# A fused layer norm, linear attention and ReLU block: w1 held in three column parts, w2 and wo loaded inside the last chunk, and two groups of sums moved

## The chip, the cores and the metric

The kernel runs on one core of a Trainium2 chip. The metric is the device time of one execution in microseconds (us). The kernel before took 221.77 us in the median of 3 runs (221.74 to 221.9). One more execution was profiled; every row of a profile below comes from that one.

The engines are named as in the profile: PE is TensorE's matmul, PEld its weight load, DVE is VectorE, ACT is ScalarE, POOL is GpSimd, SP is SyncE, which here only issues DMAs. "SPq" and "ACTq" are the DMA issues of SP and of ACT. Each engine works through its own list of instructions in order; a waiting instruction holds up everything behind it in that list.

## The reference

x has 2048 tokens of D = 640 channels. H = 32 heads of 20 channels, Dff = 1728.

```python
xn = layernorm(x)
q, k, v = split(xn @ wqkv)                # 32 heads of 20 each
phi = lambda t: where(t > 0, t + 1, exp(t)) + 1e-6
kv  = einsum("bhsd,bhse->bhde", phi(k), v)
z   = phi(k).sum(over tokens)
num = einsum("bhqd,bhde->bhqe", phi(q), kv)
den = einsum("bhqd,bhd->bhq", phi(q), z) + 1e-6
s   = (num / den) @ wo
g   = silu(relu(xn @ w1) @ w2)
out = x + s * g
```

## The kernel before, in words

**Tiles and chunks.** The tokens are 16 tiles of 128 (`t`), and four chunks of 512 (`j`). xn is kept with tokens in the partitions (`xn`) and, transposed, with channels in the partitions (`xnT`; chunk 0 has its own copy, `xcT`). From tile 4 on the transposed copy is a DMA transpose that SP issues (L497), right behind the tile's normalisation.

**The main loop (L854).** For each chunk there is a written list of blocks, `plans[j]`: an H block (`H_block`, L579) computes 128 columns of relu(xn @ w1) for the chunk, a Q block (`Q_block`, L558) 128 columns of phi(q). Each is 5 matmuls of 128 x 512. An H block's result goes through ACT (L586); a Q block's through ACT (exponential, L567) and two operations of DVE (L568, L570). At fixed positions `n` of the list other work is hung in:

- `lnat`: the statistics of a token tile (L426, L430 on DVE, then two small POOL operations, L432 and L434, that make 1/sqrt as `rsy`), and one position later its normalisation (L445 on DVE) and its transposed copy. Tiles 8 to 11 are treated in chunk 1, tiles 12 to 15 in chunk 2, at n = 0, 2, 4 and 6.
- `kat`: the key product of a token tile (`K_mm`, L507, 10 matmuls), two ACT operations (L524) and `K_fin` on DVE (L540, L542), which gives phi(k), `pk`. Tile 12's key product stands at n = 6 of chunk 2.
- `zfrom`: from which position on one addition to the running sum z (L518 on POOL, 128 x 640 in f32) is issued per position, for each `pk` that is ready. Before: from 9, 11 and 10 in chunks 0, 1 and 2.
- In chunk 3: the split of z in two bf16 halves (`z_split`, L674 and L676 on POOL), `z_col` (L681 on PE), the 64 columns of w1 left over (`H_half`, L601), and `den` (L694 on PE, then L698 and the reciprocal L703 on DVE, and four DMAs that write the reciprocal, spread over 20 channels per head, to a DRAM scratch `scr`, L709).

**The memory product.** Instead of kv directly, the kernel forms G = xn^T @ pk over all tokens (640 x 640). 128 rows of it are plain matmuls (L1154); the other 512 rows are two products of 2 x 2 blocks with seven block products instead of eight each (`seven`, L798; matmuls in L786). These need sums of the blocks of pk, called T1 to T4 (`g_T1` to `g_T4`), and of the blocks of xn, S1 to S4 for each of the two products (`g_S(0, i)`, `g_S(1, i)`). All of them are DVE operations of one helper line, L732: T of 128 x 2560, S of 128 x 1024. T3 and S3 are written over parts of pk and xn that the plain matmuls L1154 read. L821 is a DVE operation inside each `seven`.

**After it.** G is turned into kv with wv (`kv_group`, L926, evacuated by L936 on DVE), then multiplied with wo (`W_block`, L948), copied by ACT (L952) and put in place by small DMAs (L959, by SP for even blocks, by ACT for odd ones). Between these stand the first products with w2 (`U_sub`, L983). The gate's silu on ACT is L992 and L998. Before the attention output of a token tile (L1098) comes, `divide` (L725 on DVE) multiplies phi(q) by the reciprocals read back from `scr` (`load_recip`, L720, five loads of 512 KB into `Rr[0..4]`). Six more pairs of token tiles then go through `seven` with w2, the attention product, L1086, the sum with x and the store.

**Shared room.** `reg5` holds w1 and later w2. `reg7` holds the tiles of x, later the S sums of the second product, later wo. `regE` holds the work tiles of K and Q, then z's halves and the reciprocal, and later `Rr[0..3]`. Before the change w1 is one array of 5 x 1728 per partition, so that any chunk of w2 overlaps columns of all parts of w1: w2 was loaded after the last H work of the loop (`extra=[lastW1]`).

**Order and waits.** `Sched` records every operation in program order, with the keys it reads and writes; it appends it to its engine's list and derives the waits. `hz(keys)` gives the earlier users of keys whose room is used anew. A DMA waits in the list of the engine that issues it. The SP list after the loop was, before: the four stores of the reciprocal, two large and two small loads of w2, the five loads of the reciprocal, six loads of wo (`extra=[lastG]`, behind the last matmul of the second `seven`), the DMAs L959, the reload of x.

Of the kernel before, what the change touches and what calls it, by code (L numbers as in the profile page):

```python
# [208 lines left out]
def bass_recurrent_scan__linear_attn_block__dense_activation_relu__prompt_kernel(  # L209
# [9 lines left out]
    Bb, S, D = A_x.shape  # L219
# [49 lines left out]
    reg5 = nc.alloc_sbuf_tensor("reg5", [P, R5], bf)  # L269
    w1_sb = reg5[:, 0:C * FF].rearrange("p (c n) -> p c n", c=C)  # L270
    w2_sb = reg5[:, 0:NK * D].rearrange("p (c n) -> p c n", c=NK)
# [81 lines left out]
    TS = 2  # L353
    FC = [0, 4 * P, 7 * P, FF]

    def w1_part(f):
        return 0 if f < 4 else 1 if f < 7 else 2

    def w1_load(i, E):
        w_load(w1_sb[:, :, FC[i]:FC[i + 1]], B_w1[:, FC[i]:FC[i + 1]], ("w1", i), E=E)  # L360

# [217 lines left out]
    def H_block(j, f):  # L579
        b = nextb()  # L580
        src, keys = hsrc(j)
        a = sc.group("PE", [(lambda eng, k=k: eng.matmul(ps[b], lhsT=w1_sb[:, k, P * f:P * (f + 1)],  # L582
                                                         rhs=src[:, k, :],
                                                         start=(k == 0), stop=(k == C - 1))) for k in range(C)],
                     R=[("w1", w1_part(f))] + keys, W=[("ps", b)])
        sc.op("ACT", lambda eng: eng.activation(out=hT[:, f, schunk(j)], in_=ps[b], func=ACTF.Relu),  # L586
              R=[("ps", b)], W=[("hT", j, f)])
        return a

    def H_half(jp):  # L590
# [5 lines left out]
        for k in range(C):  # L596
            for u in range(2):
                src = hsrc(2 * jp + u)[0]
                for q in range(2):
                    r = 64 * u + 32 * q  # L600
                    fns.append(lambda eng, k=k, src=src, q=q, r=r: eng.matmul(  # L601
                        ps[b][r:r + 32, :], lhsT=w1_sb[:, k, NF * P + 32 * q:NF * P + 32 * (q + 1)],
                        rhs=src[:, k, :], start=(k == 0), stop=(k == C - 1), tile_position=(0, r)))
# [85 lines left out]
    def den():  # L689
# [14 lines left out]

        sc.op("DVE", frec, R=[("denS",)], W=[("rden",)])
        for i in range(J):
            src = rden[H * i:H * (i + 1), :].unsqueeze(1).to_broadcast([H, DH, 512])
# [8 lines left out]

    def load_recip():
        ex = hz([("rden",), ("denS",), ("zhi",), ("zlo",)] + ekeys + [("xcT", q, h) for q in range(4) for h in range(2)])
        for m in range(C):
            dma("SP", lambda eng, m=m: eng.dma_start(Rr[m], scr[P * m:P * (m + 1), :]),  # L720
                R=[("scr", i) for i in range(J)], W=[("Rr", m)], extra=ex)
# [37 lines left out]
    def g_Sv(pr, i):  # L759
        if i == 3:  # L760
            return xnh[:, 0:GH, P * (2 * pr + 1):P * (2 * pr + 2)]
        q = {1: 0, 2: 1, 4: 2}[i]
        base = reg6h[:, C * D:] if pr == 0 else reg7h
        return base[:, GH * P * q:GH * P * (q + 1)].rearrange("p (t n) -> p t n", t=GH)

    def g_S(pr, i):
        k0, k1 = slice(P * 2 * pr, P * (2 * pr + 1)), slice(P * (2 * pr + 1), P * (2 * pr + 2))
        xl, xh = [("xn", t) for t in range(GH)], [("xn", t) for t in range(GH, T)]
        A11, A12, A21, A22 = xn[:, 0:GH, k0], xn[:, GH:T, k0], xn[:, 0:GH, k1], xn[:, GH:T, k1]
        ex = hz([("wk", k) for k in range(C)]) if pr == 0 else hz([("xin", q) for q in range(XR)])  # L770
        key = lambda q: ("gS", pr, q)
# [26 lines left out]
    def seven(base, prod, out, mids):  # L798
# [36 lines left out]
        out(21, bd)  # L835

    lastW1 = None
    plans = [
# [6 lines left out]
    for j in range(1, J):  # L845
        ql = list(qs[j])
        for f in range(NF):
            plans[j].append(("h", j, f))
# [3 lines left out]
    lnat = [{}, {0: 8, 3: 9, 6: 10, 9: 11}, {0: 12, 2: 13, 4: 14, 6: 15}, {}]  # L852
    zfrom = [9, 11, 10, 0]
    for j in range(J):  # L854
        for n, item in enumerate(plans[j]):
# [27 lines left out]
            if n >= zfrom[j] and zpend and j < J - 1:  # L883
                z_add()
            if j == 2 and n == 0:
                g_T1()
            if j == 2 and n == 1:
                build_consts()
            if j == J - 1:
# [4 lines left out]
                if 4 <= n < 8:  # L894
                    g_S(0, n - 3)
                if n == 9:
                    z_col()
                    w_load(wv_sb[:, :, :], A_wqkv[:, 2 * D:3 * D], ("wv",), extra=hz([("zacc",)]))
                if n == 11:
                    lastW1 = H_half(0)  # L900
                    lastW1 = H_half(1)
                    den()
                if n == 12:
                    g_T2()
                    g_T4()

    for a in range(2):
        c0, c1 = (0, KH) if a == 0 else (KH, NF)
        dma("SP", lambda eng, c0=c0, c1=c1: eng.dma_start(
            w2_sb[:, c0:c1, :], B_w2[P * c0:P * c1, :].rearrange("(c p) n -> p c n", p=P)),  # L910
            W=[("w2", a)], extra=[lastW1])
    for u in range(2):
        dma("SP", lambda eng, u=u: eng.dma_start(w2_sb[64 * u:64 * (u + 1), NF, :], B_w2[NF * P:FF, :]),
            W=[("w2", 2 + u)], extra=[lastW1])
    load_recip()
    w2keys = [("w2", i) for i in range(4)]

# [234 lines left out]
    for t in range(T):  # L1152
        for a in range(2):
# [106 lines left out]
```

## Time and profile before

| | before |
|---|---|
| median of 3 runs | 221.77 us (221.74 to 221.9) |
| the profiled execution | 221.37 us |
| its span | 220.1 us |
| PE busy | 209.9 us (95%) |
| DVE busy | 146.2 us (66%) |
| ACT busy | 102.8 us (47%) |
| POOL busy | 46.1 us (21%) |
| granted TensorE clock | 1.00 |

The span runs from the first to the last recorded event. A row of the timeline gives start, duration, engine, line, operation, output<-inputs, size and how many instructions are merged in it; in brackets, how long the engine was idle before it and what ended the idle time. The table of waits sums the same brackets. A mean over the span hides where the engines meet: PE is busy 95% of it, and DVE, at 66%, was busy 15.86 of the 16.3 us from 48.7 to 65.0.

### The profile page before, as it was taken

To read this page: it belongs to the slowest core of one execution; us is meant where nothing else is said; L and a number is where in the kernel's file an instruction comes from. 1 tells how busy PE (TensorE), PEld (TensorE's weight loads), DVE (VectorE), ACT (ScalarE), POOL (GpSimd) and SP (SyncE) were. 2 spreads that over 40 slices of the span, in tenths; PEclk is the share of its full clock that TensorE was granted. 3 is DMA by queue.
4 is the path that set the end of the run, shared out by engine and by line. 5 is a ranking of instruction groups with operands and counts; after the bars stand their busy time and mean duration, and the time that the engine had idled before them with its cause. 6 is when DMAs were issued, how large, how long until landed. Compare 5 with 4: busy or idle time off the path is not lost.

```text
span 220.1 us, 3544 instructions
## 1 busy us (share of the span) xinstructions
PE 209.9 (95%) x1402; PEld 129.9 (59%) x1402; DVE 146.2 (66%) x265; ACT 102.8 (47%) x187; POOL 46.1 (21%) x70
## 2 busy tenths in 40 slices
PE   8999999999996899999999996799999999999994
PEld 7755554555542455444457675576777777777773
DVE  3899957789999891386657110995057879575254
ACT  5697575666654466655632333333332323242330
POOL 2278501229759344600000000000000000000001
PEclk9999999999999999999999999999999999999999
DMA  6987593111001120040069999525911111010002
GB/s 216 370 231 162 131 277 66 30 30 30 3 1 30 34 56 3 0 149 3 0 150 222 248 339 388 209 78 171 359 50 61 44 49 58 5 60 31 30 33 89
DMA packets 28438, 24.73 MB, mean 112 GB/s; under 512 B 12037, under 2 KB 27781, under 8 KB 28421
## 3 DMA queue, kind: packets, MB, share of 16 engines
q1 hardware_dynamic: 26335, 21.87, 35.3%
q10 hardware_dynamic: 2086, 2.63, 3.7%
q8 instruction: 11, 0.18, 0.4%
q14 instruction: 6, 0.05, 0.1%
HBM read 15.81 MB, written 5.24 MB: 96 GB/s over the span
## 4 chain that ended last, share of the span: by engine, by line
PE 72%; DVE 15%; DMA 5%; issue 2%; ACT 2%; ACTq 1%; POOL 1%
PE psT L786 23%; PE psT L582 18%; PE psT L1098 9%; PE psT L507 8%; PE psT L560 4%; DMA reg<-in_A_wo_dram 4%; DVE regE L568 3%; DVE pqT L570 3%; PE psT L983 3%; DVE reg L732 2%; PE psT L1154 2%; DVE reg L445 2%; PE psT L396 2%; DVE stats L426 1%; ACT reg L952 1%
## 5 line engine op out<-in xcount | busy, mean ns | idle before, releaser
L582 PE MATMUL psT<-reg 128*128 128x512 bf16 x195 | 46.0, 379 | 0.0
L586 ACT ACTIVATE regH<-psT 128x512 bf16<-128x512 f32 x52 | 30.8, 602 | 17.2 <-PE psT L582 17.2
L786 PE MATMUL psT<-reg 128*128 128x320 f16 (+1 forms) x238 | 34.6, 299 | 0.3 <-DVE psT L821 0.3
L582 PEld LDWEIGHTS psT<-reg 128*128 128x128 bf16 x195 | 18.9, 98 | 21.9 <-issue 0.4
L786 PEld LDWEIGHTS psT<-reg 128*128 128x128 f16 (+1 forms) x238 | 23.2, 98 | 9.6 <-DVE psT L821 0.6
L1091 POOL TENSOR_TENSOR reg<-reg 128x224 bf16<-128x224 bf16 x1 | 0.6, 606 | 124.3 <-DVE reg L1086 124.3
L518 POOL TENSOR_TENSOR wv_sb<-wv_sb,reg 128x640 f32<-128x640 f32 x16 | 23.2, 1450 | 13.4 <-DVE reg L542 12.9
L786 PE MATMUL psT<-reg,regH 128*128 128x320 bf16 (+1 forms) x168 | 24.9, 299 | 0.0
L560 PE MATMUL psT<-reg 128*128 128x512 bf16 x100 | 24.8, 379 | 0.0
L1098 PE MATMUL psT<-reg,pqT 128*128 128x320 bf16 (+2 forms) x165 | 24.2, 295 | 0.0
L998 ACT ACTIVATE wv_sb<-psT 128x320 bf16<-128x320 f32 x20 | 8.7, 437 | 27.9 <-PE psT L786 24.5
L524 ACT ACTIVATE regE<-psT 128x640 bf16<-128x640 f32 x24 | 15.6, 701 | 11.8 <-PE psT L507 11.8
L507 PE MATMUL psT<-reg 128*128 128x320 bf16 x120 | 18.3, 299 | 2.5 <-DMA reg<-reg 2.5
L786 PEld LDWEIGHTS psT<-reg,regH 128*128 128x128 bf16 (+1 forms) x168 | 16.4, 98 | 6.4
L732 DVE TENSOR_TENSOR reg<-reg 128x1024 f16<-128x1024 bf16 (+4 forms) x16 | 16.8, 1066 | 4.2 <-PE psT L1154 4.0
L1098 PEld LDWEIGHTS psT<-reg,pqT 128*128 128x128 bf16 x165 | 16.1, 98 | 5.8
L983 PE MATMUL psT<-reg,regH 128*128 128x320 bf16 x112 | 16.2, 299 | 1.8 <-DMA reg<-in_B_w_dram 1.8
L1086 DVE TENSOR_TENSOR reg<-psT,wv_sb 128x640 bf16<-128x640 f32 (+2 forms) x16 | 11.7, 739 | 9.2 <-PE psT L1098 9.2
L570 DVE SCALAR_TENSOR_TENSOR pqT<-regE 128x512 bf16<-128x512 bf16 x20 | 17.1, 856 | 0.7
L507 PEld LDWEIGHTS psT<-reg 128*128 128x128 bf16 x120 | 11.7, 98 | 9.2 <-DMA reg<-reg 3.0
L568 DVE TENSOR_SCALAR regE<-psT 128x512 bf16<-128x512 f32 x20 | 13.5, 677 | 5.2 <-ACT regE L567 5.1
L560 PEld LDWEIGHTS psT<-reg 128*128 128x128 bf16 x100 | 9.8, 98 | 11.6
(83 smaller groups left out, 244.6 us busy)
## 6 DMA issues: line engine op xcount, KB each, us to landing
scr<-regE SPq DMA_DIRECT2D x4, 640.0 KB, 8.7
reg<-in_A_x_dram SPq DMA_DIRECT2D x4, 640.0 KB, 6.6
out_dram<-reg SPq DMA_DIRECT2D x15, 160.0 KB, 1.8
reg<-in_A_x_dram SPq DMA_DIRECT2D x14, 160.0 KB, 3.3
regE<-scr SPq DMA_DIRECT2D x4, 512.0 KB, 11.6
reg<-in_B_w_dram SPq DMA_DIRECT2D x1, 1120.0 KB, 14.4
reg<-in_B_w_dram ACTq DMA_DIRECT2D x1, 1040.0 KB, 6.6
reg<-in_B_w_dram SPq DMA_DIRECT2D x1, 960.0 KB, 15.8
```

What stands on the lines that cost most here:

```text
L507: fns.append(lambda eng, a=a, k=k, lhs=lhs: eng.matmul(ps[b + a][:, 0:HN], lhsT=lhs, rhs=wk[:, k, HN * a:HN * (a + 1)], start=(k == 0), st ...
L518: sc.op("POOL", lambda eng: eng.tensor_tensor(out=zacc, in0=zacc, in1=pk[:, t, :], op=ALU.add), R=[("zacc",), ("pk", t)], W=[("zacc",)])
L524: sc.op("ACT", lambda eng: eng.activation(out=o_.rearrange("p (a n) -> p a n", a=2), in_=ps2(b, HN), func=func, scale=scale), R=[("ps", b) ...
L560: sc.group("PE", [(lambda eng, k=k: eng.matmul(ps[b], lhsT=wq[:, k, P * f:P * (f + 1)], rhs=xnT[:, j, k, :], start=(k == 0), stop=(k == C ...
L568: sc.op("DVE", lambda eng: eng.tensor_scalar(out=r_, in0=ps[b], scalar1=0.0, scalar2=1e-6, op0=ALU.max, op1=ALU.add), R=[("ps", b), ("er_e ...
L570: sc.op("DVE", lambda eng: eng.scalar_tensor_tensor(out=pqT[:, f, schunk(j)], in0=e_, scalar=1.0, in1=r_, op0=ALU.min, op1=ALU.add), R=[(" ...
L582: a = sc.group("PE", [(lambda eng, k=k: eng.matmul(ps[b], lhsT=w1_sb[:, k, P * f:P * (f + 1)], rhs=src[:, k, :], start=(k == 0), stop=(k = ...
L586: sc.op("ACT", lambda eng: eng.activation(out=hT[:, f, schunk(j)], in_=ps[b], func=ACTF.Relu), R=[("ps", b)], W=[("hT", j, f)])
L732: sc.op("DVE", lambda eng: eng.tensor_tensor(out=out, in0=in0, in1=in1, op=op), R=R, W=W, extra=extra)
L786: sc.group("PE", [(lambda eng, k=k: eng.matmul(ps[b][:, 0:HN], lhsT=lf(k), rhs=rf(k), start=(start and k == 0), stop=(k == nk - 1), skip_g ...
L983: sc.group("PE", [(lambda eng, f=f: eng.matmul(ps[b][:, 0:HN], lhsT=hT[:, f, tok(t)], rhs=w2_sb[:, f, HN * n:HN * (n + 1)], start=(f == 0) ...
L1098: sc.group("PE", [(lambda eng, c=c: eng.matmul(ps[b][:, 0:hi - lo], lhsT=pqT[:, c, tok(t)], rhs=wf[:, c, lo:hi], start=(c == 0), stop=(c = ...
```

## The change

1. w1 is kept as three arrays, one behind the other in `reg5`, for the columns of H blocks 0 to 3, 4 to 6, and 7 to 12 with the remainder. Each part covers exactly the room of w2's row chunks 0 to 3, 4 to 6, and 7 to 13.
2. In the last chunk the H blocks run in the order 7 to 12, then 0 to 6. w2 is loaded in that chunk: chunks 7 to 13 behind `H_half`, 0 to 3 behind H block 3, 4 to 6 after the loop.
3. The stores of the reciprocal (`den_store`) are issued after the last load of w2, then the loads of `Rr[3]` and `Rr[4]`; `Rr[0..2]` are loaded after the second `seven`.
4. wo is loaded at n = 1 of the last chunk, behind the last normalisation. The S sums of the second product go to `regE` instead of `reg7`.
5. `g_T1` moves from n = 0 of chunk 2 to n = 10 of chunk 3, behind `z_col`.
6. `zfrom` of chunk 1 becomes 99: its eight z additions are issued in chunk 2 from n = 10 on (and the rest at the start of chunk 3), with the four of that chunk.
7. `g_T3` moves behind the four S sums of the second product.

```diff
     R5 = max(C * FF, NK * D)
-    w1_sb = reg5[:, 0:C * FF].rearrange("p (c n) -> p c n", c=C)
+    FC = [0, 4 * P, 7 * P, FF]
+    w1_p = [reg5[:, C * FC[i]:C * FC[i + 1]].rearrange("p (c n) -> p c n", c=C) for i in range(3)]
...
+    def w1_col(k, c0, n):
+        i = w1_part(c0 // P)
+        return w1_p[i][:, k, c0 - FC[i]:c0 - FC[i] + n]
+
     def w1_load(i, E):
-        w_load(w1_sb[:, :, FC[i]:FC[i + 1]], B_w1[:, FC[i]:FC[i + 1]], ("w1", i), E=E)
+        w_load(w1_p[i], B_w1[:, FC[i]:FC[i + 1]], ("w1", i), E=E)
...
-        a = sc.group("PE", [(lambda eng, k=k: eng.matmul(ps[b], lhsT=w1_sb[:, k, P * f:P * (f + 1)],
+        a = sc.group("PE", [(lambda eng, k=k: eng.matmul(ps[b], lhsT=w1_col(k, P * f, P),
...
         sc.op("DVE", frec, R=[("denS",)], W=[("rden",)])
+    def den_store():
         for i in range(J):
...
-    def load_recip():
-        ex = hz([("rden",), ("denS",), ("zhi",), ("zlo",)] + ekeys + [("xcT", q, h) for q in range(4) for h in range(2)])
-        for m in range(C):
+    def load_recip(ms):
+        ex = hz([("rden",), ("denS",), ("zhi",), ("zlo",)] + ekeys + [("gS", 1, q) for q in (1, 2, 4)] +
+                [("xcT", q, h) for q in range(4) for h in range(2)])
+        for m in ms:
             dma("SP", lambda eng, m=m: eng.dma_start(Rr[m], scr[P * m:P * (m + 1), :]),
...
-        base = reg6h[:, C * D:] if pr == 0 else reg7h
+        base = reg6h[:, C * D:] if pr == 0 else regEh[:, 2 * D:]
...
-        ex = hz([("wk", k) for k in range(C)]) if pr == 0 else hz([("xin", q) for q in range(XR)])
+        ex = hz([("wk", k) for k in range(C)]) if pr == 0 else hz([(e_, q) for q in range(1, NEK) for e_ in ("ek_e", "ek_r")])
...
+    def w2_load(c0, c1):
+        if c0 < NF:
+            dma("SP", lambda eng: eng.dma_start(
+                w2_sb[:, c0:c1, :], B_w2[P * c0:P * c1, :].rearrange("(c p) n -> p c n", p=P)),
+                W=[("w2", c0)], extra=hz([("w1", w1_part(c0))]))
+        else:
+            for u in range(2):
+                dma("SP", lambda eng, u=u: eng.dma_start(w2_sb[64 * u:64 * (u + 1), NF, :], B_w2[NF * P:FF, :]),
+                    W=[("w2", NF, u)], extra=hz([("w1", 2)]))
...
-        for f in range(NF):
+        for f in (range(NF) if j < J - 1 else [7, 8, 9, 10, 11, 12, 0, 1, 2, 3, 4, 5, 6]):
...
-    zfrom = [9, 11, 10, 0]
+    zfrom = [9, 99, 10, 0]
...
-            if j == 2 and n == 0:
-                g_T1()
...
+                if n == 1:
+                    for c in range(VC):
+                        r0 = VR * c if c < VC - 1 else D - P
+                        dma("SP", lambda eng, c=c, r0=r0: eng.dma_start(wo_sb[:, c, :], A_wo[r0:r0 + P, :]),
+                            W=[("wo", c)], extra=[last_norm[0]])
...
                     den()
+                    w2_load(KH, NF)
+                    w2_load(NF, NK)
+                if n == 10:
+                    g_T1()
                 if n == 12:
                     g_T2()
                     g_T4()
-
-    for a in range(2):
-        c0, c1 = (0, KH) if a == 0 else (KH, NF)
-        dma("SP", lambda eng, c0=c0, c1=c1: eng.dma_start(
-            w2_sb[:, c0:c1, :], B_w2[P * c0:P * c1, :].rearrange("(c p) n -> p c n", p=P)),
-            W=[("w2", a)], extra=[lastW1])
...
-    load_recip()
+                if n == 14:
+                    w2_load(0, 4)
+
+    w2_load(4, KH)
+    den_store()
+    load_recip((3, 4))
...
-    g_T3()
     for i in range(1, 5):
         g_S(1, i)
+    g_T3()
     seven(4, gprod(0), gout(0), {})
     seven(0, gprod(1), gout(1), {})
     lastG = ("PE", sc.count["PE"] - 1)
-    for c in range(VC):
-        r0 = VR * c if c < VC - 1 else D - P
-        dma("SP", lambda eng, c=c, r0=r0: eng.dma_start(wo_sb[:, c, :], A_wo[r0:r0 + P, :]),
-            W=[("wo", c)], extra=[lastG])
+    load_recip((0, 1, 2))
```

More of the change, by code (lines that the diff above doesn't have):

```diff
@@ L353, in bass_recurrent_scan__linear_attn_block__dense_activation_relu__prompt_kernel @@
     TS = 2
-    FC = [0, 4 * P, 7 * P, FF]
     def w1_part(f):
         return 0 if f < 4 else 1 if f < 7 else 2
+    def w1_col(k, c0, n):
+        i = w1_part(c0 // P)
+        return w1_p[i][:, k, c0 - FC[i]:c0 - FC[i] + n]
     def w1_load(i, E):
-        w_load(w1_sb[:, :, FC[i]:FC[i + 1]], B_w1[:, FC[i]:FC[i + 1]], ("w1", i), E=E)
+        w_load(w1_p[i], B_w1[:, FC[i]:FC[i + 1]], ("w1", i), E=E)
     def wk_load(k0, k1):
@@ L601, in H_half @@
                     fns.append(lambda eng, k=k, src=src, q=q, r=r: eng.matmul(
-                        ps[b][r:r + 32, :], lhsT=w1_sb[:, k, NF * P + 32 * q:NF * P + 32 * (q + 1)],
+                        ps[b][r:r + 32, :], lhsT=w1_col(k, NF * P + 32 * q, 32),
                         rhs=src[:, k, :], start=(k == 0), stop=(k == C - 1), tile_position=(0, r)))
@@ L905, in bass_recurrent_scan__linear_attn_block__dense_activation_relu__prompt_kernel @@
                     g_T4()
-    for a in range(2):
-        c0, c1 = (0, KH) if a == 0 else (KH, NF)
-        dma("SP", lambda eng, c0=c0, c1=c1: eng.dma_start(
-            w2_sb[:, c0:c1, :], B_w2[P * c0:P * c1, :].rearrange("(c p) n -> p c n", p=P)),
-            W=[("w2", a)], extra=[lastW1])
-    for u in range(2):
-        dma("SP", lambda eng, u=u: eng.dma_start(w2_sb[64 * u:64 * (u + 1), NF, :], B_w2[NF * P:FF, :]),
-            W=[("w2", 2 + u)], extra=[lastW1])
-    load_recip()
-    w2keys = [("w2", i) for i in range(4)]
+                if n == 14:
[3 more added lines that the diff above has]
+    load_recip((3, 4))
+    w2keys = [("w2", KH), ("w2", NF, 0), ("w2", NF, 1), ("w2", 0), ("w2", 4)]
     gtk = [("GTq", k, n) for k in range(C) for n in range(2)]
```

## The prediction

> **What bounds the kernel now.** I read the waits of TensorE first, then the order of time on the other engines around each wait. The first lines are all waits of TensorE, but for the one at its start (total us, times, longest).
>
> ```profile
> PE psT L507 <- DMA reg<-reg: 2.5, 1, 2.5
> PE psT L983 <- DMA reg<-in_B_w_dram: 1.8, 1, 1.8
> PE psT L948 <- DMA reg<-in_A_wo_dram: 1.3, 1, 1.3
> ...
> PE psT L948 <- ACT reg L952: 0.4, 1, 0.4
> PE psT L786 <- DVE psT L821: 0.3, 1, 0.3
> ```
>
> TensorE sets the time: five waits, 6.3 us in all, are what an unchanged list of matmuls could still lose. The change adds and removes no matmul, so its worth is how many of these waits end and what new one comes.
>
> The largest stands in the third chunk (j = 2), where the key product of tile 12 waits for that tile's transposed copy. In order of time, per engine (start, duration; in brackets the idle time before):
>
> ```profile
> 72.12 1.53 PE L507 MATMUL psT<-reg 128*128 128x320 bf16 x10 [2.50 <-DMA reg<-reg]
> ...
> 58.88 1.30 ACT L524 ACTIVATE regE<-psT 128x640 bf16<-128x640 f32 x2 [0.76 <-PE psT L507]
> ...
> 64.27 0.60 ACT L567 ACTIVATE regE<-psT 128x512 bf16<-128x512 f32 x1 [0.48 <-PE psT L560]
> ```
>
> ```profile
> 40.26 0.45 DVE L445 TENSOR_SCALAR reg<-reg,mv,rsy 128x640 bf16<-128x640 bf16 x1 [0.99 <-POOL rsy L434]
> ...
> 48.83 1.51 DVE L445 TENSOR_SCALAR reg<-reg,mv,rsy 128x640 bf16<-128x640 bf16 x1 [0.99 <-POOL rsy L434]
> ...
> 62.97 0.32 DVE L540 TENSOR_SCALAR regE<-regE 128x640 bf16<-128x640 bf16 x1
> 63.33 0.49 DVE L542 TENSOR_TENSOR reg<-regE 128x640 bf16<-128x640 bf16 x1
> 63.74 0.88 DVE L426 BATCH_NORM_STATS2 stats<-reg 128x6 f32<-128x320 bf16 x2
> 64.65 0.21 DVE L430 BATCH_NORM_AGGREGATE mv<-stats 128x2 f32<-128x12 f32 x1
> 64.78 1.86 DVE L732 TENSOR_TENSOR reg<-reg 128x2560 f16<-128x2560 bf16 x1
> 66.57 0.68 DVE L568 TENSOR_SCALAR regE<-psT 128x512 bf16<-128x512 f32 x1
> 67.28 0.69 DVE L570 SCALAR_TENSOR_TENSOR pqT<-regE 128x512 bf16<-128x512 bf16 x1
> 67.89 1.59 DVE L445 TENSOR_SCALAR reg<-reg,mv,rsy 128x640 bf16<-128x640 bf16 x1
> ```
>
> ```profile
> 39.35 0.22 POOL L432 TENSOR_SCALAR rsv<-mv 128x1 f32<-128x1 f32 x1 [4.68 <-DVE mv L430]
> ...
> 48.76 9.56 POOL L518 TENSOR_TENSOR wv_sb<-wv_sb,reg 128x640 f32<-128x640 f32 x6
> ...
> 66.81 0.57 POOL L434 TENSOR_TENSOR rsy<-rsv,mhalf 128x1 f32<-128x1 f32 x1
> 67.32 1.80 POOL L403 MEMSET regH<- 128x2048 bf16 x1
> ```
>
> VectorE runs late here: tile 12's statistics (L426, L430) are followed by the moved sum T1 (L732, 1.86), the Q block's two operations, and only then the normalisation (L445), at 67.89. The same L445 takes 0.45 alone and 1.51 or 1.59 beside a GpSimd z addition (L518) or memset: both moved items, T1 and the z additions of j = 1, lie on this path.
>
> **A: T1 and the z additions leave the path to tile 12.** Without z additions in j = 1, VectorE's own work from 48.83 to tile 11's K_fin is one norm, five Q pairs and two K_fin: 0.45 + 5 x 1.37 + 2 x 0.81 = 8.9 us, ending at 57.8. What holds it then is ScalarE, whose last exponential of j = 1 ends before 58.88: the last pair ends by 60.25. K_fin of tile 11 (its inputs end at 58.88 + 1.30 = 60.18) ends by 61.1, the statistics by 62.2, the two small GpSimd operations (0.22 + 0.57, estimated 0.2 between them) by 63.1, and the memset by 64.9. The Q block's exponential ends at 64.27 + 0.60 = 64.87 as before; L568 and L570 end at 66.2, the norm, now beside no memset, at 66.7. From norm end (67.89 + 1.59 = 69.48) to matmul (72.12) the copy took 2.64, so tile 12 is there at 69.3. TensorE is free at 72.12 - 2.50 = 69.6. The wait of 2.50 goes, with 0.3 to spare. The other end: the small selects after the memset hold L570 and the norm for one lock each, as at 48.83 (1.51 - 0.45 = 1.06 twice); the wait is then 2.1 - 0.3 = 1.8, and the gain 0.7. I take 2.50, because the memset is what stood beside the 1.59 and it has moved away; the later norms of j = 2 come forward with TensorE.
>
> T1 itself, 1.86, goes to chunk j = 3 behind zmat. That slot exists: VectorE idled 3.23 before `denS`. Uncovered it would cost 1.86 less the idle time, so nothing.
>
> ```profile
> 106.21 0.69 DVE L698 TENSOR_SCALAR regE<-psT 128x512 f32<-128x512 f32 x1 [3.23 <-PE psT L694]
> ...
> 117.12 4.15 DVE L732 TENSOR_TENSOR reg<-reg 128x2560 f16<-128x2560 bf16 x5 [3.96 <-PE psT L1154]
> ```
>
> The z additions, eight of j = 1 with the four of j = 2, now all stand behind the last rsy on GpSimd. Behind them wait the split of z, then `z_col` on TensorE and, behind that, everything.
>
> ```profile
> 77.14 0.75 POOL L434 TENSOR_TENSOR rsy<-rsv,mhalf 128x1 f32<-128x1 f32 x1
> ...
> 91.72 1.40 POOL L676 TENSOR_TENSOR regE<-wv_sb,regE 128x640 bf16<-128x640 f32 x1
> ```
>
> ```profile
> 100.23 0.39 PE L681 MATMUL psT<-ones,regE 128*128 128x1 bf16 x10
> ```
>
> rsy of tile 15 ended at 77.9; 2.5 earlier is 75.4. Twelve additions at the pace of the six (9.56 / 6 = 1.59) take 19.1, the split's two operations about 2.2 (the second is 1.40, the first an estimated 0.8): z is split at 96.7. `z_col` starts at 100.23 - 2.5 = 97.7. Cost nothing, cover 1.0 us; it fails above (97.7 - 75.4 - 2.2) / 12 = 1.675 us per addition, and each further 0.1 costs 1.2.
>
> The Trainium skill (SBUF — State Buffer, "SBUF: two separate sides") speaks against this step: VectorE and GpSimd arbitrate for one port pair by an exclusive lock held for the whole instruction, and the loser blocks fully. If a locking 0.69 VectorE operation came between any two additions of about 1.40, the pace would be 2.1 and `z_col` would wait 5; by that the sum of all parts comes to about 221. The six additions ran beside blocked VectorE operations (L445 at 1.51) and still kept 1.59, so the trace shows the lock but a smaller price.
>
> **B: w2 in parts.** The wait of L983 goes if w2 lands earlier. The first line below ends the H blocks, the second is the waiting matmul; then the landing times (min/median/max) of the two large old w2 loads, which stood behind four stores of the reciprocal:
>
> ```profile
> 112.57 4.51 PE L1154 MATMUL psT<-reg 128*128 128x320 bf16 x32
> ...
> 134.58 2.08 PE L983 MATMUL psT<-reg,regH 128*128 128x320 bf16 x14 [1.81 <-DMA reg<-in_B_w_dram]
> ```
>
> ```profile
> DMA to landing us min/median/max: 14.4/15.1/15.8
> ```
>
> The last part now waits only for the last H block of TensorE (112.6 - 2.5 = 110.1) and stands ahead of those stores. At the slowest row, 15.8, it lands at 125.9; the first use is at 134.58 - 1.81 - 2.8 = 130.0 (2.8 is what A and D give). Gain 1.81 at both ends. The stores behind it start near where they did.
>
> Of the reciprocal's loads (landing min/median/max below), three now wait for the last product of the second seven and issue at about 129 to 130.5.
>
> ```profile
> DMA to landing us min/median/max: 10.6/12.0/13.6
> ```
>
> ```profile
> 145.89 1.43 DVE L725 TENSOR_TENSOR pqT<-pqT,regE 128x512 bf16<-128x512 bf16 x4
> ...
> 158.27 0.50 DVE L821 TENSOR_TENSOR psT<-psT,reg 128x320 f32<-128x320 f32 x1 [6.20 <-PE psT L786]
> ```
>
> At 13.6 they land by 144.1, while the divisions could begin at 145.89 - 5.6 = 140.3: VectorE may wait 3.8, and has 6.2 idle before TensorE next needs it. Cost nothing; uncovered it would be up to 3.8.
>
> **C: wo in the last chunk.** It issues behind the last transpose on SP (six issues); behind it stands only wv, which waits for the split and is used 30 us later. The wait of 1.3 goes, but look at what follows it:
>
> ```profile
> 140.03 0.79 ACT L992 ACTIVATE wv_sb<-psT,rsy 128x640 bf16<-128x640 f32 x1 [5.49 <-PE psT L983]
> 141.81 1.30 ACT L952 ACTIVATE reg<-psT 120x640 bf16<-120x640 f32 x2 [0.98 <-PE psT L948]
> 143.14 1.87 ACTq L959 DMA_DIRECT2D reg<-reg  x2
> 145.06 1.30 ACT L952 ACTIVATE reg<-psT 120x640 bf16<-120x640 f32 x2 [1.95 <-PE psT L948]
> ...
> 147.79 0.80 ACT L992 ACTIVATE wv_sb<-psT,rsy 128x640 bf16<-128x640 f32 x1 [1.44 <-PE psT L948]
> ```
>
> ```profile
> 141.32 0.86 PE L948 MATMUL psT<-reg 128*120 128x320 bf16 x4 [1.32 <-DMA reg<-in_A_wo_dram]
> ...
> 149.23 0.45 PE L948 MATMUL psT<-reg 128*128 128x320 bf16 x2 [0.44 <-ACT reg L952]
> ```
>
> From 141.81 to 149.23 ScalarE is one unbroken chain: copies, issues, copies, issues (in the gap shown), gate, copy. It used the wait to finish the first gate (140.03, 0.79). Without it, W block 0 runs at the gate's own start and the first copy begins at the gate's end, 0.83 after the W block instead of 0.49: the chain is 0.34 later against TensorE, and the last wait grows from 0.44 to 0.78. Gain 1.32 - 0.34 = 0.98. Ends: 0.53, if the whole gate of 0.79 is added to the chain; 1.76, if both waits vanish. I take 0.98: each step has its row.
>
> **D: T3 behind the sums.** The five operations at 117.12 (T3, four S sums) all stood behind L1154. Now the first two S sums need no product of L1154 and fall into the 3.96 idle; the wait of 0.3 goes. The other end is no gain. I take 0.30.
>
> **Sum.** 2.50 + 1.81 + 0.98 + 0.30 = 5.59. The profiled execution took 221.37 us: 215.78. The median of the runs is 0.40 above it: 221.77 - 5.59 = 216.18, so 216.2. Lowest terms, 0.7 + 1.8 + 0.5 + 0, give 218.8; highest, 2.5 + 1.8 + 1.76 + 0.3, 215.4.
>
> **The rivals.** (1) Half of A: L570 or the norm still meets a GpSimd operation and 1.06 is lost, less the 0.3 to spare: 216.9. For it: 0.3 is little cover, and several selects follow the memset. Against: beside these selects the trace shows no stretched VectorE operation. (2) C is eaten: ScalarE's chain, not wo, sets the last W block and only 0.53 comes of it: 216.6. For it: the unbroken chain; against: only the gate is new in it. (3) Slower: the late z sum. It begins to cost at 1.675 us an addition, takes the whole gain at 1.675 + 5.59 / 12 = 2.14, and at 2.2 gives 222.5; at 2.09, an addition of 1.40 and an L570 of 0.69 in turn, 221.2. For it: four K_fin and a row of Q blocks share the stretch. Against: 1.59 was the pace where VectorE was busiest. A pace between, 1.8, gives 217.7. (4) The change doesn't do what it says: T1 and z leave, but tile 12 still waits as long because its Q block's exponential is the limit; 218.7. For it: that exponential ends only at 64.87. Against: old L568 stood 1.7 behind it.
>
> **How the numbers follow.** The forecast (215.2 to 216.6) 0.62; (1) 0.14; (2) 0.08; (3) 0.09, of which 0.04 at or above the old time; (4) 0.04; unnamed, unchanged 0.03. The range 215.2 to 217.9 takes in the forecast, (1), (2) and (3) to the pace 1.8, and leaves out (4) and the far part of (3). Two measurements of this kernel are told apart from 0.2% (0.44 us): faster 0.93, same 0.03, slower 0.04.
>
> **What would show it.** In TensorE's waits after: L507 on a copy gone (A), L983 on w2 gone (B), L948 on wo gone and L948 on ScalarE near 0.8 (C), L786 on L821 gone (D). Statistics of tile 12 end near 62, the norm takes 0.45 and ends before 67. A wait of L681 on GpSimd would be (3); L507 still waiting, with L445 at 1.5, (1). It is wrong if a wait that is not in the first list sets TensorE back.

## The result, and the profile after

| | before | after |
|---|---|---|
| median | 221.75 us (4 runs, 220.39 to 221.9) | 215.07 us (4 runs, 214.65 to 215.37) |
| ratio to before, 95% interval | | 0.971 (0.967 to 0.975) |
| the profiled execution / its span | 221.37 / 220.1 us | 215.22 / 214.0 us |

The change gained 6.15 us between the two profiled executions, where 5.59 was forecast, and 6.68 between the medians. The measured 215.07 lies 0.13 below the low end of the stated range.

In the kernel after, the lines have moved: L445 is L449 (norm), L507 is L511 (key product), L518 is L522 (z addition), L568 and L570 are L572 and L574 (Q block on VectorE), L681 is L685 (`z_col`), L786 and L821 are L792 and L827 (`seven`), L948 and L952 are L967 and L971 (W block and its copy), L983 and L992 are L1002 and L1011 (product with w2 and its gate). All waits of TensorE in the kernel after (total us, times, longest):

```profile
PE psT L967 <- ACT reg L971: 0.9, 2, 0.4
PE psT L400 <- PEq L1261: 0.8, 1, 0.8
PE psT L586 <- issue: 0.2, 1, 0.2
```

The waits for the copy of tile 12, for w2, for wo and for L821 are all gone; the one on ScalarE has doubled, in two places. The wait put to "issue" is new in the list, but it is a gap in the records and costs nothing: the row holds 29 matmuls where the kernel before shows 30 (L582 at 106.09).

```profile
103.73 6.42 PE L586 MATMUL psT<-reg 128*128 128x512 bf16 x29 [0.16 <-issue]
```

The stretch before tile 12, in order of time on TensorE, VectorE and GpSimd:

```profile
68.47 1.24 PE L586 MATMUL psT<-reg 128*128 128x512 bf16 x5
69.55 1.52 PE L511 MATMUL psT<-reg 128*128 128x320 bf16 x10
```

```profile
61.68 0.21 DVE L434 BATCH_NORM_AGGREGATE mv<-stats 128x2 f32<-128x12 f32 x1
64.98 0.69 DVE L572 TENSOR_SCALAR regE<-psT 128x512 bf16<-128x512 f32 x1 [3.09 <-ACT regE L571]
65.71 0.69 DVE L574 SCALAR_TENSOR_TENSOR pqT<-regE 128x512 bf16<-128x512 bf16 x1
66.32 0.44 DVE L449 TENSOR_SCALAR reg<-reg,mv,rsy 128x640 bf16<-128x640 bf16 x1
...
82.50 1.52 DVE L544 TENSOR_SCALAR regE<-regE 128x640 bf16<-128x640 bf16 x1
84.05 1.61 DVE L546 TENSOR_TENSOR reg<-regE 128x640 bf16<-128x640 bf16 x1
```

```profile
62.80 1.80 POOL L407 MEMSET regH<- 128x2048 bf16 x1
...
74.27 19.02 POOL L522 TENSOR_TENSOR wv_sb<-wv_sb,reg 128x640 f32<-128x640 f32 x12
93.35 1.05 POOL L678 CAST regE<-wv_sb 128x640 bf16<-128x640 f32 x1
94.49 1.72 POOL L680 TENSOR_TENSOR regE<-wv_sb,regE 128x640 bf16<-128x640 f32 x1
```

VectorE now has 3.09 us of idle time before the Q pair ahead of tile 12's norm; the norm takes 0.44 and ends at 66.8, beside no memset. The price is seen further on: the twelve z additions run at 74.27 to 93.3, 1.585 each, and VectorE's K_fin operations beside them take 1.5 and 1.6. VectorE had room for that: no wait of TensorE on VectorE is left.

The table puts the gain into stages by start times of TensorE's rows (what lies between the first and the second row of the table, `z_col` in it, is unchanged in length: 40.45 before, 40.44 after):

| stage | before | after | gain | forecast |
|---|---|---|---|---|
| A: start of tile 12's key product | 72.12 | 69.55 | 2.57 | 2.50 |
| B and D: L1154 / L1173 to the first product with w2 | 112.57 to 134.58 | 109.99 to 129.55 | 2.45 | 1.81 + 0.30 |
| C: first product with w2 to the last W block | 134.58 to 149.23 | 129.55 to 143.10 | 1.10 | 0.98 |

The sum is 6.12, the difference of the spans 6.1. The after rows that the table uses, and ScalarE beside them:

```profile
109.99 4.51 PE L1173 MATMUL psT<-reg 128*128 128x320 bf16 x32
114.33 8.86 PE L792 MATMUL psT<-reg 128*128 128x320 bf16 x64
...
129.55 2.06 PE L1002 MATMUL psT<-reg,regH 128*128 128x320 bf16 x14
...
134.79 0.71 PE L967 MATMUL psT<-reg 128*120 128x320 bf16 x4
...
140.28 0.48 PE L967 MATMUL psT<-reg 128*120 128x320 bf16 x2 [0.44 <-ACT reg L971]
...
143.10 0.45 PE L967 MATMUL psT<-reg 128*128 128x320 bf16 x2 [0.43 <-ACT reg L971]
```

```profile
134.99 0.80 ACT L1011 ACTIVATE wv_sb<-psT,rsy 128x640 bf16<-128x640 f32 x1 [3.50 <-PE psT L1002]
135.68 1.29 ACT L971 ACTIVATE reg<-psT 120x640 bf16<-120x640 f32 x2
137.00 1.88 ACTq L978 DMA_DIRECT2D reg<-reg  x2
138.93 1.30 ACT L971 ACTIVATE reg<-psT 120x640 bf16<-120x640 f32 x2 [1.96 <-PE psT L967]
```

### The profile page after: what moved, and what is told of

It is laid out like the page before. It is cut to its first block, busy times and chain, and to the rows that moved or that the text cites. A ratio compares the mean times of both kernels' runs of the same rounds, so it can differ in the third digit from the quotient of the medians.

```text
span 214.0 us, 3534 instructions
## 1 busy us (share of the span) xinstructions
PE 208.5 (97%) x1392; PEld 130.2 (61%) x1402; DVE 149.7 (70%) x265; ACT 102.7 (48%) x187; POOL 46.5 (22%) x70
## 3 DMA queue, kind: packets, MB, share of 16 engines
HBM read 15.81 MB, written 5.24 MB: 98 GB/s over the span
## 4 chain that ended last, share of the span: by engine, by line
PE 92%; ACT 2%; DVE 2%; ACTq 1%; DMA 1%; issue 1%
PE psT L586 26%; PE psT L792 26%; PE psT L511 10%; PE psT L564 10%; PE psT L1117 10%; PE psT L1002 4%; PE psT L1173 2%; ACTq L978 1%; ACT reg L971 1%; DMA reg<-in_A_x_dram 1%; PE psT L605 1%; PE psT L485 1%; DVE reg L1105 1%; ACT wv_sb L1011 1%; PE psT L945 1%
## 5 line engine op out<-in xcount | busy, mean ns | idle before, releaser
L586 PE MATMUL psT<-reg 128*128 128x512 bf16 x192 | 45.5, 379 | 0.3 <-issue 0.2
L586 PEld LDWEIGHTS psT<-reg 128*128 128x128 bf16 x195 | 18.9, 98 | 21.9 <-issue 0.4
L792 PE MATMUL psT<-reg 128*128 128x320 f16 (+1 forms) x214 | 31.5, 299 | 0.0
L792 PEld LDWEIGHTS psT<-reg 128*128 128x128 f16 (+1 forms) x214 | 20.9, 98 | 8.1
L792 PE MATMUL psT<-reg,regH 128*128 128x320 bf16 (+1 forms) x168 | 24.9, 299 | 0.0
L522 POOL TENSOR_TENSOR wv_sb<-wv_sb,reg 128x640 f32<-128x640 f32 x16 | 23.8, 1489 | 2.3 <-DVE reg L546 1.3
L564 PE MATMUL psT<-reg 128*128 128x512 bf16 x95 | 23.8, 379 | 0.3
L792 PEld LDWEIGHTS psT<-reg,regH 128*128 128x128 bf16 (+1 forms) x168 | 16.4, 98 | 6.4
L572 DVE TENSOR_SCALAR regE<-psT 128x512 bf16<-128x512 f32 x20 | 13.6, 679 | 7.1 <-ACT regE L571 7.1
L511 PE MATMUL psT<-reg 128*128 128x320 bf16 x120 | 18.3, 299 | 0.0
L574 DVE SCALAR_TENSOR_TENSOR pqT<-regE 128x512 bf16<-128x512 bf16 x20 | 17.0, 851 | 0.7
L738 DVE TENSOR_TENSOR reg<-reg 128x1024 f16<-128x1024 bf16 (+4 forms) x13 | 15.0, 1163 | 2.8 <-PE psT L1173 2.7
L564 PEld LDWEIGHTS psT<-reg 128*128 128x128 bf16 x100 | 9.8, 98 | 11.6
L1002 PE MATMUL psT<-reg,regH 128*128 128x320 bf16 x112 | 16.2, 299 | 0.0
L571 ACT ACTIVATE regE<-psT 128x512 bf16<-128x512 f32 x20 | 11.9, 597 | 8.8 <-PE psT L564 8.8
```

The source lines that it names most:

```text
L511: fns.append(lambda eng, a=a, k=k, lhs=lhs: eng.matmul(ps[b + a][:, 0:HN], lhsT=lhs, rhs=wk[:, k, HN * a:HN * (a + 1)], start=(k == 0), st ...
L522: sc.op("POOL", lambda eng: eng.tensor_tensor(out=zacc, in0=zacc, in1=pk[:, t, :], op=ALU.add), R=[("zacc",), ("pk", t)], W=[("zacc",)])
L564: sc.group("PE", [(lambda eng, k=k: eng.matmul(ps[b], lhsT=wq[:, k, P * f:P * (f + 1)], rhs=xnT[:, j, k, :], start=(k == 0), stop=(k == C ...
L574: sc.op("DVE", lambda eng: eng.scalar_tensor_tensor(out=pqT[:, f, schunk(j)], in0=e_, scalar=1.0, in1=r_, op0=ALU.min, op1=ALU.add), R=[(" ...
L738: sc.op("DVE", lambda eng: eng.tensor_tensor(out=out, in0=in0, in1=in1, op=op), R=R, W=W, extra=extra)
L792: sc.group("PE", [(lambda eng, k=k: eng.matmul(ps[b][:, 0:HN], lhsT=lf(k), rhs=rf(k), start=(start and k == 0), stop=(k == nk - 1), skip_g ...
```

## The experiments

All times are medians of 6 runs of each kernel; the kernels are called x1 to x12, in the order in which they were run. They were taken on three chips (x1 to x4, x5 to x8, x9 to x12), with runs of the kernel before beside them, whose medians were 221.79, 221.75 and 221.38 us. The changed kernel itself was not run again, so a difference from 215.07 of a few tenths of a us is read from the rows of the profile where it matters. Each kernel is the changed one with one edit, unless said otherwise. None leaves out part of the computation.

**Part A, taken apart.** T1 back in its old place:

```diff
+            if j == 2 and n == 0:
+                g_T1()
...
-                if n == 10:
-                    g_T1()
```

> The changed kernel with T1 back at n = 0 of chunk 2; the z additions stay late. Theory (one path with slack): VectorE ends tile 12's statistics at 61.9 and the next exponential comes only at about 64.9, so T1 (1.8) fits between and costs nothing by itself; but it holds GpSimd's small operations back, the memset then lies over L574 and the norm ends at about 67.3 instead of 66.7. The wait of L511 is 0.2 to 0.6, the time 215.07 + 0.2 to 0.7 = 215.3 to 215.8. Rival (T1's own duration is what the old wait was made of): T1 costs its 1.8 again less the slack of 0.3, the wait is about 1.5 and the time about 216.6.

Measured (x1): 215.2 us, and no wait of L511 on the copy. T1 (1.44 here) ran at 61.99 in the idle time, held GpSimd's small operation up (L436 took 1.35), and cost nothing. It came out slightly better than the theory's 0.2 to 0.7, since the memset ended at 65.91, ahead of the norm at 66.50, which took 0.49. With the z additions out of the way, T1 needed no moving.

The z additions back in their old place:

```diff
-    zfrom = [9, 99, 10, 0]
+    zfrom = [9, 11, 10, 0]
```

> The changed kernel with the z additions of chunk 1 back in chunk 1; T1 stays in chunk 3. Theory (one path with slack): tile 12's statistics end at 64.9 as before the change, its rsy at about 66.2, the Q pair at about 66.2 too; the memset then starts before the norm and the norm is held, 1.5 instead of 0.45, and ends near 67.8. The wait of L511 is 0.7 to 1.2, the time 215.07 + 0.9 to 1.4 = 216.0 to 216.5. Rival (T1 alone made the wait): no wait returns, 215.1. Rival (the z additions alone made it): the whole 2.5 returns, 217.7.

Measured (x2): 216.31 us. VectorE, GpSimd and TensorE of this kernel around the norm:

```profile
65.93 2.01 DVE L449 TENSOR_SCALAR reg<-reg,mv,rsy 128x640 bf16<-128x640 bf16 x1
```

```profile
65.27 0.57 POOL L438 TENSOR_TENSOR rsy<-rsv,mhalf 128x1 f32<-128x1 f32 x1
65.78 1.80 POOL L407 MEMSET regH<- 128x2048 bf16 x1
```

```profile
68.09 1.24 PE L586 MATMUL psT<-reg 128*128 128x512 bf16 x5
70.59 1.53 PE L511 MATMUL psT<-reg 128*128 128x320 bf16 x10 [1.26 <-DMA reg<-reg]
```

The norm starts at 65.93, just after the memset has begun, and takes 2.01: it ends at 67.94, 0.36 after the memset (67.58), as if its own 0.44 came only then. That a norm held by the memset makes the wait was the theory; the next kernel tests it by moving the memset too (z additions back as here):

```diff
-            if j == 2 and n == 1:
+            if j == 2 and n == 8:
                 build_consts()
```

> The z additions of chunk 1 back in chunk 1, as in x2_z_back, and the constants (the memset of 1.8 and the selects) built at n = 8 of chunk 2 instead of n = 1. Theory (in x2_z_back the norm of tile 12 was held by that memset, 2.01 instead of 0.45): the norm takes 0.45 from about 65.9, the copy is there at 69.0, no wait of L511, 215.07. Rival (the z additions themselves keep tile 12 late): a wait near 1.26 stays, 216.3.

Measured (x11): 215.24 us, no wait of L511, and the norm is short:

```profile
65.92 0.44 DVE L449 TENSOR_SCALAR reg<-reg,mv,rsy 128x640 bf16<-128x640 bf16 x1
```

So the z additions in j = 1 do not by themselves keep tile 12 late once T1 is gone. With T1 gone they delay its statistics just enough for GpSimd's memset to fall on the norm. Both back, all of A undone:

> The changed kernel with T1 and the z additions both back: all of part A undone, w2, wo and T3 as changed. Theory (parts add up, each wait worth its printed length and about 0.15 for the matmul that no longer overlaps the one before): the wait of L511 is 2.5 again and the time 215.07 + 2.65 = 217.7. Rival (a wait is worth its printed length): 217.57. Rival (later waits took up part of it): under 217.0.

Measured (x3): 217.92 us; the old wait is back (2.49 us), and nothing later took up any of it. The two do not add up: T1 alone costs 0.1 (not told apart from nothing), the z additions alone 1.2, both 2.85 (in two of these six executions, 219.12 and 219.14 us, the granted clock was 0.992; in the others, 217.53 to 218.05, it was 1.00). The other way round, the kernel before with A alone (T1 to n = 10 of j = 3, z as in the change):

> The kernel before with T1 and the z additions moved and nothing else: part A alone. Theory (parts add up): the wait of L511 is gone, those of L983 on w2 (1.8), of L948 on wo (1.3), on ScalarE (0.4) and of L786 (0.3) stay; 221.75 - 2.65 = 219.1. Rival (w2's and wo's landing times are set by a queue that does not come forward): w2 and wo land when they did, the waits grow by what A gave, and the time is 220.5 or more.

Measured (x4): 218.48 us. Its other waits are those of before, almost to the tenth:

```profile
PE psT L983 <- DMA reg<-in_B_w_dram: 1.7, 1, 1.7
PE psT L948 <- DMA reg<-in_A_wo_dram: 1.4, 1, 1.4
...
PE psT L948 <- ACT reg L952: 0.4, 1, 0.4
PE psT L786 <- DVE psT L821: 0.3, 1, 0.3
```

All loads moved forward together with TensorE, as the theory has it; the median is 0.6 below the expected 219.1. The expected time started from 221.75, a median over executions of unequal granted clock: beside x4 the kernel before took 220.35 to 221.07 us in its four executions at 1.00, and 221.62 or more in the seven at 0.992 or less. All six with A alone had 0.998 or more. Taken from the four, 2.65 less is 217.7 to 218.4, and most of the 0.6 is accounted for.

**Part B.** All of w2 behind the stores of the reciprocal again, w1 still in parts:

```diff
+    den_store()
+    w2_load(0, 4)
     w2_load(4, KH)
-    den_store()
+    w2_load(KH, NF)
+    w2_load(NF, NK)
     load_recip((3, 4))
```

> The changed kernel with all of w2 loaded behind the stores of the reciprocal, as before the change: part B undone. Theory (w2 was late because it stood behind four slow stores): it lands about as long after them as before, the wait of L1002 is 1.5 to 1.9 and costs 0.15 more; 215.07 + 1.7 to 2.1 = 216.8 to 217.2. Rival (w2 was late because five reciprocal loads and wo shared the queues behind it; only two of them do now): w2 lands in 5 to 8 us, no wait, 215.1.

Measured (x5): 216.73 us. The matmul waits, but 1.30 rather than the 1.5 to 1.9 expected:

```profile
130.80 2.08 PE L1001 MATMUL psT<-reg,regH 128*128 128x320 bf16 x14 [1.30 <-DMA reg<-in_B_w_dram]
```

The three large loads landed after (min/median/max) the first line's times here, and after the second line's in the changed kernel:

```profile
DMA to landing us min/median/max: 11.4/12.1/12.7
```

```profile
DMA to landing us min/median/max: 3.9/4.2/5.4
```

Neither story has all of it. The stores ahead are most of the delay, since 12 us stay with only two reciprocal loads behind instead of five; the other 3 us (the load of 960 KB landed after 12.7 here and 15.8 before) fit the loads that used to follow, but no run changes only those. Then the counter-test: all of w2 issued behind the main loop, but ahead of the stores:

```diff
-                    w2_load(KH, NF)
-                    w2_load(NF, NK)
...
-                if n == 14:
-                    w2_load(0, 4)
...
+    w2_load(0, 4)
     w2_load(4, KH)
+    w2_load(KH, NF)
+    w2_load(NF, NK)
     den_store()
```

> The changed kernel with all of w2 loaded after the last H block, in one go, but ahead of the stores of the reciprocal; nothing comes part by part. Theory (the place ahead of the stores is what B is worth): 2.2 MB issued at about 110 land by 120 at the rate of the after profile's loads (5 us each), the first use is at 129.5, no wait, 215.07. The stores and the two loads that follow them move by some 5 us and are not needed before 140. Rival (the parts are what makes w2 early): w2 is late again and L1002 waits 1 or more, 216.2 or more; or the reciprocal's loads come late and VectorE holds TensorE near 152.

Measured (x10): 214.98 us, no wait for w2. One of the three large loads still came early: w1 is in parts here too, so the load of w2's row chunks 0 to 3 was issued at 106.91, ahead of the end of the last H block at about 110, and the third at 110.6. But the slowest of the three landed in 6.5 us, and the first use is at about 129.5: with one w1 array and all loads issued from 110 on, w2 would be there well before 120, an estimate from these landing times. So what B gains is w2's place ahead of the stores, and the three parts of w1, which give the change its name, are worth nothing that these runs show. No run has one w1 array and w2 ahead of the stores.

**Part C.** wo behind the second seven and the reciprocal's loads again:

```diff
-                if n == 1:
-                    for c in range(VC):
-                        r0 = VR * c if c < VC - 1 else D - P
-                        dma("SP", lambda eng, c=c, r0=r0: eng.dma_start(wo_sb[:, c, :], A_wo[r0:r0 + P, :]),
-                            W=[("wo", c)], extra=[last_norm[0]])
...
     load_recip((0, 1, 2))
+    for c in range(VC):
+        r0 = VR * c if c < VC - 1 else D - P
+        dma("SP", lambda eng, c=c, r0=r0: eng.dma_start(wo_sb[:, c, :], A_wo[r0:r0 + P, :]),
+            W=[("wo", c)], extra=[lastG])
```

> The changed kernel with wo loaded behind the second seven and the three reciprocal loads: part C undone. Theory (ScalarE's chain from the first copy to the last W block is the path; it used the wait for its gate): wo lands at 134.5 to 136.5, TensorE waits up to 1.5 for it, but the waits on ScalarE at the last two W blocks shrink by 0.3 to 0.8; in all 0 to 1.1 is lost: 215.1 to 216.2, and the last W block starts 7.9 after the first. Rival (the wait for wo is lost in full beside the others): the last two W blocks wait 0.44 and 0.43 still, and the time is 215.07 plus the whole wait and 0.15.

Measured (x6): 216.53 us, 0.3 above the expected 216.2; the six executions lie between 216.06 and 218.69, and the median by itself would also fit the rival. The rows decide. Those of TensorE (the profiled execution lost about 1.9 us in its first 10, from a wait of 0.51 for `wqkv` on, so lengths are read and not times):

```profile
131.41 2.06 PE L997 MATMUL psT<-reg,regH 128*128 128x320 bf16 x14
...
138.19 0.88 PE L962 MATMUL psT<-reg 128*120 128x320 bf16 x4 [1.38 <-DMA reg<-in_A_wo_dram]
...
146.10 0.45 PE L962 MATMUL psT<-reg 128*128 128x320 bf16 x2 [0.44 <-ACT reg L966]
```

From the first product with w2 to the last W block: 14.69, against 13.55 with wo early. A wait of 1.38 came and one of two waits on ScalarE went; 1.14 is lost and not the full wait, as the theory has it. From the first W block to the last it takes 7.91, as in the kernel before (149.23 - 141.32). ScalarE's chain was tested from its own side by giving all its DMA issues to SP:

```diff
-            dma("ACT" if c % 2 else "SP", lambda eng, q=q, e=e: eng.dma_start(wf[q % P:q % P + e - q, q // P, :],
+            dma("SP", lambda eng, q=q, e=e: eng.dma_start(wf[q % P:q % P + e - q, q // P, :],
```

> The changed kernel with all the small DMAs behind the W blocks issued by SP; in it ScalarE issues those of every second block. Theory (ScalarE's chain of copies, issues and gate is what the last two W blocks wait for): without 1.9 + 1.4 us of issues the chain is never behind, both waits (0.44 and 0.43) go with about 0.15 each of lost overlap, and the time is 215.07 - 1.1 = 213.9 to 214.1. Rival (the pieces then stand in one list on SP and land too late): a new wait of L1117 on these DMAs, 215 or more. Rival (the chain is the copies themselves): the waits stay, 215.07.

Measured (x9): 213.81 us (213.55 to 214.13), ratio to before 0.967 (0.962 to 0.971): the fastest of all, 1.26 us below the changed kernel, whose runs do not overlap with its own. All waits of its TensorE, and the rows from the first product with w2 to the last W block:

```profile
PE psT L400 <- PEq L1261: 0.8, 1, 0.8
PE psT L586 <- issue: 0.2, 1, 0.2
```

```profile
129.60 2.06 PE L1002 MATMUL psT<-reg,regH 128*128 128x320 bf16 x14
...
141.91 0.43 PE L967 MATMUL psT<-reg 128*128 128x320 bf16 x2
```

From the first of these rows to the last it takes 12.31, against 13.55 in the changed kernel: 1.24 less, within one execution each. The issues of 1.88 and 1.35 us were the part of the chain that held the last two W blocks. SP had the time, and the pieces still land before they are used.

**Part D.** T3 ahead of the S sums again:

```diff
+    g_T3()
     for i in range(1, 5):
         g_S(1, i)
-    g_T3()
```

> The changed kernel with T3 ahead of the four S sums again: part D undone. Theory (a printed wait of 0.3 is worth 0.45, since the matmul behind it no longer overlaps): L792 waits 0.3 on L827 again and the time is 215.07 + 0.45 = 215.5. Rival (worth its printed length): 215.37. Rival (hidden anyway): 215.07.

Measured (x7): 215.42 us, 0.35 more, which by itself does not tell 0.30 from 0.45. Its rows do:

```profile
114.14 4.51 PE L792 MATMUL psT<-reg 128*128 128x320 bf16 x32
118.96 4.52 PE L792 MATMUL psT<-reg 128*128 128x320 f16 x32 [0.30 <-DVE psT L827]
...
129.84 2.06 PE L1002 MATMUL psT<-reg,regH 128*128 128x320 bf16 x14
```

From the first L792 to the product with w2 it takes 15.70, against 129.55 - 114.33 = 15.22 in the changed kernel: a printed wait of 0.30 costs 0.48.

**The cover of the late z sum.** The memset of 1.8 us on GpSimd repeated ahead of the additions, twice and once:

```diff
+            if j == 2 and n == 9:
+                sc.allow_unread.add(("hz",))
+                for _ in range(2):
+                    sc.op("POOL", lambda eng: eng.memset(hT[:, NF, :], 0.0), W=[("hz",)])
```

> The changed kernel with GpSimd's memset of the last H rows done twice more (two of 1.8 us) ahead of the late z additions; this is extra work, the result is the same. Theory (the late z sum has 1.4 us of cover before z_col): z is split at 96.2 + 3.6 = 99.8, z_col, which stood at 97.64, waits 2.1 to 2.4 and the time is 215.07 + 2.2 to 2.5 = 217.3 to 217.6. Rival (something else covers z_col too, such as the matmuls already queued, or GpSimd catches up): under 216.

Measured (x8): 219.08 us. The wait is the expected one, but in the median 1.5 us more were lost. TensorE, and the granted clock of the stretches behind (the column behind the five busy times):

```profile
100.36 0.39 PE L685 MATMUL psT<-ones,regE 128*128 128x1 bf16 x10 [2.44 <-POOL regE L680]
100.61 3.61 PE L586 MATMUL psT<-reg 128*128 128x512 bf16 x10
```

```profile
97.50:100.30 2.80, 0.42 (x2) 0.00 (x0) 2.77 (x3) 0.60 (x1) 2.64 (x2) 1.00 0.00 0
100.30:102.00 1.70, 1.64 (x16) 0.92 (x17) 1.67 (x3) 0.00 (x0) 0.00 (x0) 0.85 0.37 38
102.00:105.00 3.00, 3.00 (x18) 0.84 (x20) 2.96 (x6) 1.19 (x2) 0.00 (x0) 0.52 0.70 252
105.00:110.00 5.00, 4.84 (x65) 2.15 (x59) 2.64 (x3) 2.96 (x5) 0.00 (x0) 1.00 0.38 105
```

Behind the wait TensorE was granted 0.85 and then 0.52 of its clock for some 3 us; the ten matmuls at 100.61 took 3.61 where 2.32 is their time in the kernel before. Not every execution shows it: in four of the six the granted clock over the span was 0.990 to 0.992 (219.03 to 219.6 us), in two it was 1.00, and these took 217.63 and 217.97, close to the expected 217.3 to 217.6. Once only:

> As x8_z_late with one more memset (1.8) instead of two. Theory (cover of z_col 1.4, each us beyond costs one, and the slow clock seen after the 2.4 us wait of x8_z_late needs the long wait): z is split at about 98.1, z_col waits 0.6, the granted clock stays at 1.00, and the time is 215.07 + 0.6 + 0.15 = 215.8. Rival (any wait there brings the slow clock): about 217.

Measured (x12): 215.62 us, a wait of 0.55, the granted clock at 1.00 in the stretches around it:

```profile
98.14 0.39 PE L685 MATMUL psT<-ones,regE 128*128 128x1 bf16 x10 [0.55 <-POOL regE L680]
```

So the late z sum had some 1.4 us of cover (96.2 to 97.64), and beyond it each microsecond costs one as long as the clock holds.

## Why the prediction came out as it did

**A** held: statistics at 61.9 (62.2 was the bound), norm 0.44 ending at 66.8 (66.7), copy in time, wait gone. That T1 and the z additions both lay on the path is true of the kernel before, but the wait is not a sum of two shares: moving the z additions alone would have ended it (x1), moving T1 alone would have left 1.26 of it (x2). In these runs T1 costs something only when the z additions have already made VectorE late, and the z additions without T1 cost something only through the memset, which then falls on tile 12's norm (x11).

**The z sum** came out nearly to the digit in its pace: 1.585 per addition against 1.59, and no wait of `z_col`. That the split was ready at 96.2, close to the 96.7 foreseen, is in part luck: at 2.9 us it took 0.7 more than estimated, but the additions began at 74.3 instead of 75.4. The rule of the Trainium skill that spoke against this step (SBUF — State Buffer, "SBUF: two separate sides": an exclusive lock, the loser blocked fully) is borne out for VectorE, whose K_fin operations took 1.5 to 1.6 instead of 0.3 to 0.5. The trace does not agree with a pace of 2.1: GpSimd lost only 0.19 per addition beside them.

**B** was right in the gain, and too careful in the landing: 3.9 to 5.4 us, where the bound used 15.8. So the margin was not 4 us but over 10. The three reciprocal loads behind the second `seven` cost nothing, as forecast.

**C** was right in its mechanism: the chain on ScalarE took back part of what wo's wait had cost. The first copy starts 0.89 after the W block (135.68 against 134.79), where 0.83 was foreseen, and from the first W block to the last it takes 8.31 instead of 7.91: 0.40 is taken back, where 0.34 was foreseen. The last wait was put at 0.78 in one place; it stands in two, 0.44 and 0.43, since W block 4 also waits for a copied bank.

**D** held: the wait of 0.30 is gone.

**The term that was mis-sized** is what a wait is worth. The sum took each wait at its printed length, the idle time in the brackets of its row. The rows of the changed kernel show why that is too little: L586 at 68.47 lasts 1.24, yet the next group starts 1.08 later. A group of matmuls overlaps the end of the one before by 0.16, and a wait loses this too. The row ahead of the old wait of 2.50:

```profile
68.39 1.24 PE L582 MATMUL psT<-reg 128*128 128x512 bf16 x5
```

From here to the key product at 72.12 it takes 3.73, against 1.08 in the changed kernel, so a printed 2.50 cost 2.65. In x2 the printed 1.26 cost 70.59 - 68.09 - 1.08 = 1.42, and the runs show 0.48 for a wait of 0.30. Part by part, measured less forecast:

- A: 2.57 - 2.50 = 0.07. The wait gave 0.15 more, but the changed kernel's profiled execution was already 0.08 later when it came there.
- B and D: 2.45 - 2.11 = 0.34, of which D has 0.18 and B, at 1.97 for 1.81, 0.16.
- C: 1.10 - 0.98 = 0.12. From the first product with w2 to the first W block 6.74 became 5.24, so the wait of 1.32 was worth 1.50, 0.18 more; the chain took back 0.06 more.

Together they make 0.53 of the 0.56 us that the forecast missed between the profiled executions. That is half of the 1.1 us between the forecast 216.2 and the measured 215.07, and the four mechanisms stand.

The other 0.5 us between the medians' difference (6.68) and the profiled one (6.15) has a likely source that the forecast did not reckon with, the granted clock. On the three chips of the experiments the kernel before was executed 34 times. In 13 of them the granted clock was 0.998 or more, and they took 219.97 to 221.38 us; in 21 it was 0.992 or less, and they took 221.28 to 224.97. The profiled execution, 221.37, had 1.00, and all four of the changed kernel had 0.999 or more. For the other executions behind the median of before no clock is on record, so this is not shown for them.

## What to carry to other kernels

Before splitting a buffer to load earlier, look at what stands ahead of the load in its issuing engine's list: here four stores were most of the delay, and the order, not the parts, was worth the 2 us. Where a wait is removed, follow the chain that ran in its shadow on the other engines; the issues of small DMAs on a busy engine can be the next limit, and moving them to an idle one gave 1.3 us more. When two pieces of work seem to share a late path, put each back alone before giving either a share. For the price of a TensorE wait, measure from start to start: here it was about 0.16 us longer than the idle time shown. And compare executions of the same granted clock, since a wait can change it.

## What the runs showed of the hardware

**A wait can cost clock.** Behind a wait of 2.44 us of `z_col` the granted clock fell to 0.52 for about 3 us, which made the wait some 1.5 us dearer; behind the wait of 2.50 of the kernel before, in its profiled execution, it stayed at 1.00. The Trainium skill (TensorE: Matmul & The Clock Gate, "Part 1: The HAM clock gate") puts the fall behind an idle window of about 3.4 us that runs freely; a wait of 2.44 was enough in this profile, and what sets the two apart is not settled by these runs. They do show that it goes by execution, and mostly with such a wait. A granted clock of 0.992 or less came in 21 of 34 executions of the kernel before (longest wait 2.50), in 2 of 6 of x3 (2.49) and in 4 of 6 of x8 (2.44); of the 64 executions of the other eleven kernels, whose longest wait is 1.7, it came in one, of x6 (1.38). Only for x8 does a profile show where in the span the clock fell.

**An issue takes longer behind other transfers.** SP issued each large w2 load in 0.37 to 0.38 us in the changed kernel (L845). In x5, behind the four stores, the same three loads took 1.9 to 2.1 us each to issue, 6.15 in all:

```profile
113.38 6.15 SPq L845 DMA_DIRECT2D reg<-in_B_w_dram  x3
```
